# Retention attention and a top-2 router on one core: decay moved from the outputs to q and k, a router cut into thirty steps

## The chip, the cores and the metric

The kernel runs on one core of one Trainium2 chip. The time is that of the device in microseconds (us), from one launch to its end. The profiler takes one more execution, which is longer than a plain one; its times are used here to see where time goes, not how much there is of it.

The engines have short names: PE is TensorE's matmul, PEld its weight load, DVE is VectorE, ACT is ScalarE, POOL is GpSimd, SP is the engine that issues most DMAs. Each engine runs its own list of instructions in order and waits for the others through semaphores.

## The reference

The attention part has 8 batches, 8 heads, 576 positions, 64 wide. The mixture of experts takes its output as 4608 tokens of 512.

```python
scores = q @ k.T / 8                                  # per batch and head
gamma  = 1 - 2 ** (-5 - head)
Dmat   = where(i >= j, gamma ** (i - j), 0)           # i: query position, j: key position
x      = (scores * Dmat) @ v                          # -> [4608, 512]

noisy  = x @ w_gate + log1p(exp(x @ w_noise)) * noise
top2   = the two largest of 8 experts for each token; weights = softmax over the two
out[t] = sum over the two experts e of weight * relu(x[t] @ w1[e]) @ w2[e]
```

The decay `gamma ** (i - j)` splits into a factor for the query and a factor for the key, so it needs no matrix of its own: only the mask `i >= j` has to be applied to the scores.

## The kernel before, in words

**Attention.** The work is cut into 16 units: a unit is half of the heads (four) of one batch, 512 of the 576 positions; four units make a group, which is two batches with all heads (1152 tokens). The last 64 positions of both batches of a group form a "tail", done after the units of the same heads. The loop over `n` from 0 to 16 has a unit `u = n` that begins and a unit `p = n - 1` that ends. Its calls, in order, are: scores of the first pair of heads (`scores(u, 0)`), the output of the unit before (`out(p)`), the transposes of the next unit's q (`tr(u + 1, "q")`), the scores of the second pair, the cast of unit `u + 2` (`cast`), the transposes of the next k, the scores of the tail where there is one (`scores_tail`), the running states of the unit (`states`), and the output of the tail (`out_tail`). Raw q, k and v come from memory four units ahead.

**Casts.** The float32 inputs become bf16 in `cast`: k on POOL by two `affine_select` (L194), v on POOL by a product with a table of key decays (L199), q on ACT with the factor 1/8 (L203). The tails do the same (`cast_tail`, L215 to L221). The query's decay is put on at the end: `out` multiplies what stands in PSUM with the table `gt` on DVE as it copies it to `xT` (L326), two instructions in each unit; `out_tail` does so for the tail (L351).

**Scores.** PE writes the scores of two heads to two PSUM tiles of the name `S` (of which there are just two buffers), and DVE multiplies each with the mask as it copies it out (L270). `scores_tail` takes buffers of the same name, one for each head, one after the other (L336, L337).

**Router.** At the end of each group `route(bp)` begins. It is a generator: each call of `step()` in the attention loop (seven in a pass) lets it run to its next `yield`, so its instructions are put between those of the attention on every engine's list. It computes the gate logits on PE (L489), copies them (L494), takes exp and log on ACT (L496, L497), finds the two largest experts on DVE with some fifty small instructions, counts tokens for each expert (POOL L543, PE L576 and L578), builds one-hot matrices on DVE (L642 to L652), from which PE makes the lists of tokens (L658), and writes the rows of tokens with their weights to the DRAM tensor `xd` (POOL L636). Nine `row(c)` calls transpose the tokens back for that (PE L483, ACT L484). It has some twenty steps.

**Experts.** `early` computes five expert tiles (256 tokens each), for which three of the four groups are enough. It is created when the third route is done; from pass 16 on its pieces alternate with the steps of the route that still runs. When the fourth route is done, the rest of the tiles follow in `experts`, 35 of them, which is mainly a stream of matmuls (L942, L961) fed by gathers on POOL (L823).

The order of the instructions on each engine is the order of these calls: the scheduler is told to keep it for all five engines.

```python
def step():
    while pend and next(pend[0], pend) is pend:
        pend.pop(0)
        routed.append(0)
        if len(routed) == 3:
            work.append(early(tc, K, at, keep, xd, yd, W, EARLY, routed))
    if n == NU:
        more()
```

Of the kernel before, what the change touches and what calls it, by code (L numbers as in the profile page):

```python
# [16 lines left out]
P = 128  # L17
# [26 lines left out]
HD = 64  # L44
NC9 = 9
# [58 lines left out]
def decay_tables(nc, cp, tmp):  # L104

    vg = cp.tile([P, 2, 2, 4, 2], F32, name="vg")
    vgt = cp.tile([P, 8], F32, name="vgt")
    gt = cp.tile([P, 4, 576], F32, name="gt")
    tv = tmp.tile([P, 576], F32, name="tv", bufs=1)
    nc.gpsimd.iota(tv[:, :512].rearrange("p (c r q) -> p c r q", c=4, r=4), pattern=[[P, 4], [1, 4], [4, 32]],  # L110
                   base=0, channel_multiplier=0, allow_small_or_imprecise_dtypes=True)
    nc.gpsimd.iota(tv[:, 512:], pattern=[[1, HD]], base=512, channel_multiplier=0,
                   allow_small_or_imprecise_dtypes=True)
    sv = tmp.tile([P, 2, 2], F32, name="sv")
    nc.gpsimd.iota(sv, pattern=[[256, 2], [1, 2]], base=0, channel_multiplier=2,
                   allow_small_or_imprecise_dtypes=True)
    st = tmp.tile([P, 1], F32, name="st")
    for b in range(2):
        nc.gpsimd.iota(st[b * HD:(b + 1) * HD], pattern=[[0, 1]], base=512, channel_multiplier=1,
                       allow_small_or_imprecise_dtypes=True)  # L120
    for h in range(8):
        lng = math.log(1.0 - 2.0 ** (-5.0 - h))
        hp, hi = h // 2, h % 2
        s = slice(hi * HD, (hi + 1) * HD)
        nc.scalar.activation(vg[:, h // 4, :, h % 4, :], sv, Act.Exp, scale=-lng)
        nc.scalar.activation(vgt[:, h:h + 1], st, Act.Exp, scale=-lng)
        nc.scalar.activation(gt[s, hp, :], tv[s], Act.Exp, scale=lng)
    return vg, vgt, gt


class Attention:
# [26 lines left out]
    def tables(self):  # L158
        self.vg, self.vgt, self.gt = decay_tables(self.nc, self.cp, self.bf)
        for t in self.Tb:  # L160
            self.nc.gpsimd.memset(t, 0.0)
# [24 lines left out]
    def cast(self, u):  # L186

        nc = self.nc
        d = self.u[u]
        hq = self.unit(u)[1]  # L190
        kn = self.bf.tile([P, 2, 2, 4, HD], BF16, name="kn", bufs=3)
        rk = d.pop("rawk").rearrange("p c h (r d) -> p (c h) r d", r=2)
        for r in range(2):
            nc.gpsimd.affine_select(kn[:, r].rearrange("p c h d -> p (c h) d"), rk[:, :, r, :],  # L194
                                    pattern=[[0, 8], [0, HD]], base=1, channel_multiplier=0,
                                    compare_op=Alu.is_gt, fill=0.0)
        vn = self.bf.tile([P, 2, 2, 4, HD], BF16, name="vn", bufs=3)
        rv = d.pop("rawv").rearrange("p c h (r d) -> p (c h) r d", r=2)
        nc.gpsimd.tensor_tensor(vn.rearrange("p r c h d -> p (c h) r d"), rv,  # L199
                                self.vg[:, hq].rearrange("p c h r -> p (c h) r").unsqueeze(3).to_broadcast(  # L200
                                    [P, 8, 2, HD]), Alu.mult)
        qb = self.bf.tile([P, 4, 4, HD], BF16, name="qb")
        nc.scalar.activation(qb.rearrange("p r h d -> p h r d"),  # L203
                             d.pop("rawq").rearrange("p c h w -> p (c h w)").rearrange("p (h r d) -> p h r d", h=4, r=4),
                             Act.Copy, scale=0.125)
        d.update(kn=kn, vn=vn, qb=qb)

    def cast_tail(self, bp):
        nc = self.nc
        d = {}  # L210
        for n in "qk":
            t = self.bf.tile([P, DM], BF16, name=n + "t", bufs=1)
            a = self.tails.pop((n, bp)).rearrange("p h d -> p (h d)")
            if n == "q":
                nc.scalar.activation(t, a, Act.Copy, scale=0.125)  # L215
            else:
                nc.gpsimd.affine_select(t, a, pattern=[[0, DM]], base=1, channel_multiplier=0,
                                        compare_op=Alu.is_gt, fill=0.0)
            d[n] = t
        t = self.bf.tile([P, 8, HD], BF16, name="vt")  # L220
        nc.gpsimd.tensor_tensor(t, self.tails.pop(("v", bp)), self.vgt.unsqueeze(2).to_broadcast([P, 8, HD]), Alu.mult)  # L221
        d["v"] = t
        self.tails[bp] = d

    def tr_tail(self, bp):
# [3 lines left out]
        for hp in range(4):  # L229
            for j, n in enumerate("qk"):  # L230
                nc.tensor.transpose(pt[:, hp, j, :], d[n][:, hp * P:(hp + 1) * P], self.K["ident"])
# [65 lines left out]
    def out(self, u):  # L297
# [17 lines left out]
        for e in range(2):  # L315
# [9 lines left out]
            gv = self.gt[:, 2 * hq:2 * hq + 2, :512].rearrange("p y (c e t) -> p y c e t", c=2, e=2)[:, :, :, e, :]  # L325
            nc.vector.tensor_tensor(xv, p[e], gv, Alu.mult)  # L326

    def scores_tail(self, bp, hp):
        nc = self.nc
        t = self.tails[bp]  # L330
        T = t["T"][:, hp]
        S = self.sp.tile([P, 2, P], BF16, name=f"St{hp % 2}")
        for h in range(2):
            s = slice(h * HD, (h + 1) * HD)
            p = self.ps.tile([P, P], F32, name="S", bufs=2)
            nc.tensor.matmul(p, lhsT=T[s, 1, :], rhs=T[s, 0, :], start=True, stop=True)  # L336
            nc.vector.tensor_tensor(S[:, h, :], p, self.K["maskt"].rearrange("p r q -> p (r q)"), Alu.mult)  # L337
        t["S", hp] = S

    def out_tail(self, bp, hp):  # L340
        nc = self.nc
        t = self.tails[bp]
        p = self.ps.tile([P, 2, HD], F32, name="x", bufs=2)
        for h in range(2):
            s = slice(h * HD, (h + 1) * HD)
            nc.tensor.matmul(p[s].rearrange("p b t -> p (b t)"), lhsT=t["v"][:, 2 * hp + h, :], rhs=t["S", hp][:, h, :],
                             start=True, stop=False, skip_group_check=True)
        for b in range(2):
            nc.tensor.matmul(p[:, b, :], lhsT=self.T.pop((bp, b, hp))[:, 3, :], rhs=t["T"][:, hp, 0, b * HD:(b + 1) * HD],
                             start=False, stop=(b == 1), skip_group_check=True)  # L350
        nc.vector.tensor_tensor(self.xT[bp][:, hp, 8, :].rearrange("p (b t) -> p b t", b=2), p,  # L351
                                self.gt[:, hp, 512:].unsqueeze(1).to_broadcast([P, 2, HD]), Alu.mult)
# [80 lines left out]
class Router:  # L433
# [36 lines left out]
    def route(self, bp):  # L470
# [15 lines left out]
        pg = ps.tile([P, C, 2 * E], F32, name="R", bufs=1)  # L486
        for c in range(C):
            for di in range(KD):
                nc.tensor.matmul(pg[:, c, :], lhsT=xT[:, di, c, :], rhs=self.wgn[:, di, :],  # L489
                                 start=(di == 0), stop=(di == KD - 1))  # L490
            if c == 4:
                yield
        lg = sp.tile([P, C, 2 * E], F32, name="lg")
        V.tensor_copy(lg, pg)  # L494
# [3 lines left out]
        row(0)  # L498
        yield
        row(1)  # L500
        V.tensor_mul(nl[:, :8], nl[:, :8], self.noise[:, 2 * bp:2 * bp + 2].rearrange("p b c e -> p (b c) e"))
        V.tensor_mul(nl[:, 8], nl[:, 8], self.noiset[:, bp])
        V.tensor_add(nl, nl, lg[:, :, :E])
# [18 lines left out]

        m1, w1 = first_max(nl, "a")
        yield
        row(2)
# [3 lines left out]
        V.scalar_tensor_tensor(nl2, M1, -1.0e30, nl, Alu.mult, Alu.add)  # L529
        m2, w2 = first_max(nl2, "b")  # L530
        yield
        row(3)
# [11 lines left out]
        yield  # L544
        row(4)
# [4 lines left out]
        r = col("r")  # L550
        V.tensor_scalar_add(r, d, 1.0)
        V.reciprocal(r, r)
        V.tensor_mul(d, d, r)
        low1 = col("low1")
        V.tensor_tensor(low1, w1, w2, Alu.is_gt)
        df = col("df")
        V.tensor_sub(df, r, d)
        V.tensor_mul(df, df, low1)
        yield


        pl = sp.tile([P, C, PLW], F32, name="pl")
        V.memset(pl[:, :, 7], 0.0)
        V.tensor_add(pl[:, :, 1], d, df)
        V.tensor_sub(r, r, df)
        V.tensor_sub(pl[:, :, 2], r, pl[:, :, 1])
        V.tensor_scalar(pl[:, :, 0], w[:, 1], -1.0, float(E), Alu.mult, Alu.add)
        V.tensor_copy(pl[:, :, 3], K["tok"][:, bp])
# [5 lines left out]
        yield  # L574
        pr = ps.tile(SH, F32, name="R", bufs=1)
# [4 lines left out]
        row(5)  # L580
        yield

        prf = sp.tile(SH, F32, name="prf", bufs=1)
        V.tensor_tensor(prf, pr, self.fill.unsqueeze(1).to_broadcast(SH), Alu.add)
        V.tensor_mul(pd, M, prf)
        rk = sp.tile([P, C, 2], F32, name="rk")
# [5 lines left out]
        V.tensor_reduce(rc, pd, AX, Alu.add)  # L592

# [10 lines left out]
        yield  # L604
        row(6)
        lo = sp.tile([P, 2, C], BF16, name="lo")
        V.tensor_copy(lo, lh[:, 0])
        hi = sp.tile([P, 2, C], F32, name="hi")
        V.tensor_copy(hi, lh[:, 1])

        key = self.keep["key"][:, :, c0:c0 + C]
        V.tensor_scalar(key, w, -KEY, KEY * E + 1.0, Alu.mult, Alu.add)
# [611 lines left out]
```

## The time and the profile before

| what | value |
|---|---|
| time, median of 3 runs | 549.66 us (549.3 to 552.47) |
| span of the profiled execution | 597.5 us |
| PE busy | 454.6 us (76%) |
| DVE, ACT, POOL busy | 277.8, 268.2, 274.3 us (45% to 46%) |
| granted PE clock, mean | 0.847 |
| first transposes of attention | at 15.95 us |
| attention's last pass ends | at about 211 us |
| first matmuls of the remaining expert tiles | at 261 us |

The average share of an engine says little here, as the kernel has stages with different limits: 16 passes of attention with the router between them, then the last route beside the early expert tiles, then the experts. A pass can be found in the trace by its first score matmuls (L264): they start at 19.0, 28.3, 34.4, 42.0 and 48.1 us for passes 0 to 4, and at 55.4, 67.2, 87.7, 96.6 and 103.9 us for passes 5 to 9. The first route begins at the end of pass 4.

### The profile page before, as it was taken

The page shows a single profiled execution, that of the slowest core. Times are in us where ns is not written, and L with a number is a line of the kernel's source. Part 1 is how long each engine was busy: PE and PEld are TensorE (multiplying, and loading weights), DVE is VectorE, ACT ScalarE, POOL GpSimd, SP SyncE. Part 2 cuts the span into 40 slices and gives each one's busy share as a digit, 9 for nine tenths or more (in the row PEclk, how much of TensorE's full clock was granted, in tenths as well). Part 3 has the DMA queues.
Part 4 walks back from the last instruction along what each step waited for, and adds up shares of the span by engine and source line. Part 5 has one row for each costly group of instructions (what it writes and reads, how often), then busy time and mean ns, then how long its engine had stood idle before and what let it go on. Part 6 is the DMA issues. An engine that isn't in the chain of part 4 may idle for free.

```text
span 597.5 us, 11717 instructions
## 1 busy us (share of the span) xinstructions
PE 454.6 (76%) x4587; PEld 315.4 (53%) x4627; DVE 277.8 (46%) x770; ACT 268.2 (45%) x381; POOL 274.3 (46%) x350
## 2 busy tenths in 40 slices
PE   0687738828756678968998799799798798989960
PEld 0565626616644455645665366366464464656630
DVE  0266796796778278313333143243233243344430
ACT  5657716723660365534563464464444451312200
POOL 8753543335232605570246216336347256666660
PEclk9989758655875697988999699799799698999995
DMA  9995999709446313730677567577575643544450
GB/s 239 285 238 119 249 297 265 223 0 259 73 72 130 92 41 125 261 118 17 219 257 251 164 218 235 173 253 232 183 269 183 218 135 114 166 129 130 146 176 20
DMA packets 96170, 104.18 MB, mean 174 GB/s; under 512 B 25447, under 2 KB 73065, under 8 KB 96112
## 3 DMA queue, kind: packets, MB, share of 16 engines
q1 hardware_dynamic: 79824, 69.51, 39.4%
q0 software_dynamic: 15232, 32.84, 20.0%
q10 hardware_dynamic: 1056, 1.05, 0.5%
q8 instruction: 37, 0.61, 0.4%
q14 instruction: 21, 0.17, 0.1%
HBM read 84.66 MB, written 28.72 MB: 190 GB/s over the span
## 4 chain that ended last, share of the span: by engine, by line
PE 25%; issue 17%; POOL 5%; DMA 3%; DVE 2%; another core or an unknown queue 1%; POOLq 0%; ACT 0%; DVEq 0%; ACTq 0%
PE p L942 13%; PE po L961 11%; POOL xg L823 3%; DMA xg<-xd,xi 2%; PE pt L926 1%; POOL out_dram L1003 1%; POOL prv L969 1%; DVE o L997 1%; DMA raw_q<-xd,xi 0%; DMA out_dram<-o,ix 0%; DVE hT L949 0%; ACT xgT L929 0%; POOLq L823 0%; ACT hT L947 0%
## 5 line engine op out<-in xcount | busy, mean ns | idle before, releaser
L942 PE MATMUL p<-xgT,w 128*128 128x256 bf16 x1120 | 223.7, 283 | 18.2 <-issue 13.4
L961 PE MATMUL po<-w,hT 128*128 128x512 bf16 x525 | 205.3, 395 | 11.2 <-issue 9.7
L942 PEld LDWEIGHTS <-w 128*128 128x128 bf16 x1120 | 112.8, 101 | 98.8 <-issue 31.8
L949 DVE TENSOR_SCALAR hT<-p 128x512 bf16<-128x512 f32 x70 | 48.3, 691 | 195.3 <-PE p L942 106.0
L947 ACT ACTIVATE hT<-p 128x512 bf16<-128x512 f32 x70 | 41.8, 597 | 173.6 <-remote 62.9
L1003 POOL DMA_INDIRECT out_dram<-o,ix x45 | 45.7, 1016 | 113.3 <-DVE o L997 98.8
L823 POOL DMA_INDIRECT xg<-xd,xi x64 | 66.0, 1032 | 19.2 <-issue 18.6
L961 PEld LDWEIGHTS <-hT 128*128 128x128 bf16 x560 | 56.3, 100 | 26.1 <-issue 17.4
L969 POOL DMA_INDIRECT prv<-yd,ix x45 | 45.6, 1014 | 39.5 <-issue 39.5
L270 DVE TENSOR_TENSOR S<-S,mask 128x512 bf16<-128x512 f32 x64 | 41.1, 683 | 38.5 <-PE S L264 38.5
L892 ACT ACTIVATE w<-wst 128x1024 bf16<-128x1024 f32 x48 | 47.8, 1048 | 0.0
L292 ACT ACTIVATE Tb<-T 64x512 bf16<-64x512 f32 x32 | 18.8, 589 | 44.7 <-PE T L286 44.4
L194 POOL TENSOR_SCALAR_AFFINE_SELECT kn<-raw_k 128x512 bf16<-128x512 f32 x32 | 24.4, 786 | 26.5 <-issue 10.0
L929 ACT ACTIVATE xgT<-pt 128x1024 bf16<-128x1024 bf16 x35 | 35.7, 1020 | 1.6 <-PE pt L926 1.6
L199 POOL TENSOR_TENSOR vn<-raw_v,vg 128x1024 bf16<-128x1024 f32 x16 | 30.9, 1933 | 5.5 <-DMA raw_v<-in_v_dram 1.5
L997 DVE SCALAR_TENSOR_TENSOR o<-po,g,prv 128x512 f32<-128x512 f32 x45 | 31.7, 742 | 3.0 <-DMA prv<-yd,ix 1.7
L336 PE MATMUL S<-TT 64*128 64x128 bf16 x32 | 7.1, 231 | 31.4 <-DVE S L270 20.1
L543 POOL TENSOR_TENSOR cum<-cum,M 128x16 bf16<-128x16 bf16 x36 | 7.8, 217 | 49.8 <-DVE d L548 47.3
L249 PE MATMUL tr<-ident,qb 128*128 128x128 bf16 x128 | 14.1, 277 | 21.4 <-ACT qb L203 16.3
L484 ACT ACTIVATE xr<-tr 128x512 bf16<-128x512 bf16 x36 | 21.2, 598 | 12.6 <-PE tr L483 9.3
L636 POOL COPY xr<-pl 128x24 f32<-128x24 f32 x12 | 12.1, 1048 | 28.1 <-issue 18.8
L251 ACT ACTIVATE QT<-tr 128x1024 bf16<-128x1024 bf16 x16 | 16.4, 1023 | 18.9 <-PE tr L249 18.9
(205 smaller groups left out, 678.6 us busy)
## 6 DMA issues: line engine op xcount, KB each, us to landing
wst<-in_moe_w_dram SPq DMA_DIRECT2D x48, 512.0 KB
raw_k<-in_k_dram SPq DMA_DIRECT2D x32, 256.0 KB
raw_v<-in_v_dram SPq DMA_DIRECT2D x32, 256.0 KB
yd<-y SPq DMA_DIRECT2D x16, 512.0 KB
raw_q<-in_q_dram SPq DMA_DIRECT2D x14, 512.0 KB
xd<-xr SPq DMA_DIRECT2D x12, 396.0 KB
w<-in_moe_w_dram POOLq DMA_DIRECT2D x4, 1024.0 KB
yd<-raw_v SPq DMA_DIRECT2D x5, 512.0 KB
```

Of the source, the lines that this page charges most:

```text
L199: nc.gpsimd.tensor_tensor(vn.rearrange("p r c h d -> p (c h) r d"), rv, self.vg[:, hq].rearrange("p c h r -> p (c h) r").unsqueeze(3).to_b ...
L270: nc.vector.tensor_tensor(S, p[h], self.K["mask"].unsqueeze(1).to_broadcast([P, 2, 2, P]), Alu.mult)
L823: tc.nc.gpsimd.indirect_dma_start(out=xg[:, s, :], out_offset=None, in_=xd[:, :], in_offset=IOff(ap=keep["xi"][:, j:j + 1], axis=0), bound ...
L892: nc.scalar.activation(W[e][:, k * F:(k + 1) * F], t, Act.Copy)
L929: return lambda: nc.scalar.activation(xgT, pt, Act.Copy)
L942: nc.tensor.matmul(p1[:, f2, :], lhsT=w[:, o:o + P], rhs=xgT[:, di, :], start=(di == 0), stop=(di == KD - 1))
L947: nc.scalar.activation(hT[:, 2 * fp:2 * fp + 2, :], p1, Act.Relu)
L949: V.tensor_relu(hT[:, 2 * fp:2 * fp + 2, :], p1)
L961: nc.tensor.matmul(po[s], lhsT=hT[:, fi, s * P:(s + 1) * P], rhs=w[:, o:o + DM], start=(fi == 0), stop=(fi == KF - 1))
L969: nc.gpsimd.indirect_dma_start(out=prv[i % NP][:, s, :], out_offset=None, in_=yd[:rows, :], in_offset=IOff(ap=st[i]["ix"][:, s, 1:2], axis=0),
L997: V.scalar_tensor_tensor(o[:, s, :], st[i]["po"][s], st[i]["g"][:, s:s + 1], prv[i % NP][:, s, :], Alu.mult, Alu.add)
L1003: ins = nc.gpsimd.indirect_dma_start(out=out[:, :], out_offset=IOff(ap=st[i]["ix"][:, s, 0:1], axis=0), in_=st[i]["o"][:, s, :], in_offset ...
```

## The change

Four things change.

1. The query's decay is put on q, and the key's decay on k instead of v, when they are cast. Both are counted from the middle of the sequence (position 288), so that no factor becomes large. The cast of k and that of q become one product each on POOL (for the first two units on DVE), and v is only copied, on ACT. Then nothing is left to be multiplied in `out`: of the two copies from PSUM one is done by ACT and one by DVE. The large table `gt` is not needed any more.
2. The tail's scores and outputs are done for two pairs of heads at once: two DVE instructions in place of four, and one copy on ACT in place of two products on DVE.
3. The router is cut into about thirty steps, and its work is put in another order. Some small instructions go from DVE to POOL (the row's fields `pl`, the overflow keys `key`), and the one-hot matrices are made in two halves.
4. The gate weights are kept as the sum of two bf16 parts, which makes the gate logits more exact: the matmuls are 32 wide in place of 16, and DVE adds the two halves.

The tables for the decay and the zeros of `Tb` are made before the constants, and `Tb` is cleared by DVE.

```diff
     def cast(self, u, eng=None):
...
-        for r in range(2):
-            nc.gpsimd.affine_select(kn[:, r].rearrange("p c h d -> p (c h) d"), rk[:, :, r, :],
...
+        eng.tensor_tensor(kn.rearrange("p r c h d -> p (c h) r d"),
...
-        nc.gpsimd.tensor_tensor(vn.rearrange("p r c h d -> p (c h) r d"), rv,
...
+        nc.scalar.activation(vn.rearrange("p r c h d -> p (c h) r d"),
+                             d.pop("rawv").rearrange("p c h (r d) -> p (c h) r d", r=2), Act.Copy)
...
-        nc.scalar.activation(qb.rearrange("p r h d -> p h r d"),
...
+        eng.tensor_tensor(qb.rearrange("p r h d -> p h r d"),
...
     # out
-            nc.vector.tensor_tensor(xv, p[e], gv, Alu.mult)
+            if e:
+                nc.vector.tensor_copy(xv, p[e])
+            else:
+                nc.scalar.activation(xv, p[e], Act.Copy)
...
     # scores_tail, out_tail
-        for h in range(2):
-            p = self.ps.tile([P, P], F32, name="S", bufs=2)
...
+        p = [self.ps.tile([P, 2, P], F32, name="S", bufs=2) for h in range(2)]
...
-        nc.vector.tensor_tensor(self.xT[bp][:, hp, 8, :].rearrange("p (b t) -> p b t", b=2), p,
-                                self.gt[:, hp, 512:].unsqueeze(1).to_broadcast([P, 2, HD]), Alu.mult)
+        nc.scalar.activation(self.xT[bp][:, 2 * hq:2 * hq + 2, 8, :], p.rearrange("p y b t -> p y (b t)"), Act.Copy)
...
     # route
-        V.tensor_copy(lg, pg)
+        V.tensor_copy(lg, pg[:, :, 1])
+        V.tensor_add(lg, lg, pg[:, :, 0])
...
-        V.memset(pl[:, :, 7], 0.0)
-        V.tensor_add(pl[:, :, 1], d, df)
...
+        G = nc.gpsimd
+        G.memset(pl[:, :, 7], 0.0)
+        G.tensor_tensor(pl[:, :, 1], d, df, Alu.add)
...
-        V.tensor_tensor(olo.rearrange("p a c l -> p (a c) l"), K["iota"].unsqueeze(1).to_broadcast(sh),
...
+        for j in range(2):
+            sh = [P, C, P]
+            V.tensor_tensor(olo[:, j], K["iota"].unsqueeze(1).to_broadcast(sh),
...
+            yield
...
-        V.tensor_add(key, key, rc.rearrange("p c a -> p a c"))
+        G.tensor_tensor(key, key, rc.rearrange("p c a -> p a c"), Alu.add)
...
-        at.cast(0)
+        at.cast(0, nc.vector)
+        nc.gpsimd.tensor_copy(wgn[:, :, 0], wg32)
+        nc.gpsimd.tensor_tensor(wgn[:, :, 1], wg32, wgn[:, :, 0], Alu.subtract)
```

## The prediction, made before the changed kernel had run

> **What bounds the kernel now.** I read first the busy time by stage. The columns are the stretch (us), its length, then busy time and instruction count of PE, PEld, DVE, ACT and POOL, the granted PE clock, the DMA share and GB/s. The first three rows are, roughly, passes 4 to 7, 8 to 11 and 12 to 15; then come the last route and the experts:
>
> ```profile
> 49.80:98.00 48.20, 30.98 (x600) 24.77 (x598) 38.83 (x102) 26.18 (x37) 22.75 (x29) 0.72 0.97 257
> 98.00:149.00 51.00, 33.52 (x542) 26.48 (x539) 40.10 (x105) 24.96 (x36) 20.68 (x26) 0.59 0.65 166
> 149.00:201.00 52.00, 31.61 (x588) 24.78 (x586) 37.57 (x106) 22.15 (x32) 17.31 (x27) 0.70 0.51 92
> ...
> 211.00:259.00 48.00, 39.11 (x310) 26.18 (x312) 31.56 (x111) 26.42 (x44) 21.30 (x27) 0.93 0.40 138
> 259.00:597.00 338.00, 282.27 (x1925) 184.49 (x1959) 109.00 (x297) 133.00 (x177) 152.53 (x152) 0.91 0.54 176
> ```
>
> In the three stretches with a route DVE is busiest (38 to 40 us of about 50), though its share over the whole span is 46%. The experts are a PE stage, and the change doesn't touch them. So I cut the first route's stretch into its passes 5, 6, 7 and 8:
>
> ```profile
> 55.40:67.20 11.80, 8.00 (x163) 6.50 (x160) 7.43 (x25) 9.07 (x15) 4.85 (x13) 0.83 0.75 200
> 67.20:87.70 20.50, 9.01 (x147) 6.73 (x146) 19.61 (x55) 6.90 (x11) 10.94 (x12) 0.58 1.00 256
> 87.70:96.60 8.90, 8.19 (x146) 7.12 (x144) 6.82 (x12) 4.41 (x6) 5.04 (x4) 0.65 1.13 325
> 96.60:103.90 7.30, 5.90 (x156) 4.54 (x154) 5.25 (x12) 5.72 (x8) 2.83 (x3) 1.00 0.94 219
> ```
>
> DVE has 19.6 of pass 6's 20.5 us: the router's load falls into one pass. Passes 7 and 8 follow PE, with 2 us of DVE free in each. Pass 5 follows no busy engine; there ACT's list (exp, a table load of 1.28 us, log) stands ahead of the copies that PE waits for. PE's waits in passes 5 to 15 (us in total, times, longest) say the same:
>
> ```profile
> PE S L336 <- DVE S L270: 18.0, 10, 6.3
> PE S L336 <- DVE St L337: 10.3, 5, 3.3
> PE S L264 <- DVE S L270: 6.1, 6, 3.0
> PE tr L249 <- ACT xr L484: 5.2, 3, 2.1
> ```
>
> PE waits for a buffer `S` that DVE reaches late, behind router work: 34 us. Last, the timeline of pass 10 (start, us, engine, line):
>
> ```profile
> 116.14 0.58 DVE L557 TENSOR_TENSOR df<-r,d 128x9 f32<-128x9 f32 x1
> ...
> 116.68 1.90 POOL L199 TENSOR_TENSOR vn<-raw_v,vg 128x1024 bf16<-128x1024 f32 x1
> 116.75 1.85 DVE L558 TENSOR_TENSOR df<-df,low 128x9 f32<-128x9 f32 x1
> ```
>
> Nine elements take 1.85 us instead of 0.17 (the shortest of that line), and end with POOL's product: POOL's casts hold DVE up.
>
> **What the Trainium skill says.** "GPSIMD Engine Reference", Specifications: its SBUF interfaces are shared with VectorE, in contention with DVE instructions with two SBUF inputs or in a two-port mode. The trace agrees (L558 above). "VectorE: DVE Perf Modes", Why PSUM operands drop a tier: float32 from PSUM gets one element a cycle at most, so a plain copy is as dear as a product. The trace has 0.682 us for the product L326 and 0.691 for the one-input L949. "TensorE: Matmul & The Clock Gate", What's actually happening: PE's clock halves after an idle window. The trace agrees: 1.00 in pass 8, 0.58 in pass 6. So shorter waits pay a little twice; I put no number on that.
>
> **The change part by part**, for a group of four passes unless said otherwise.
>
> *Outputs.* DVE does one copy of 0.69 (row L949) in each pass instead of two of 0.682 (L326): 4 x (1.364 - 0.69) = 2.7 us less. ACT gets a copy of 0.60 (row L947) in each pass: +2.4.
>
> *Tails.* DVE's eight L337 (0.286) and four L351 (0.288) were 3.44 us. Four instructions of 256 elements remain. Between 0.286 at 128 and 0.683 at 512 elements a line gives 0.42 each, 1.67 in all: 1.8 us less. ACT gets two small copies, about 0.4 each.
>
> *Router on DVE.* Where the last route runs undisturbed, the six `pl` instructions take 0.65 us start to start (225.16 to 225.81), L631 to L633 0.38, the four `key` ones 0.88, and one of L622/L624 goes: 2.1 less. Added: one sum for the two gate halves, 0.3 (as L494); four more instructions by halving the one-hots, about 0.06 each. Net 1.5 us less. DVE so loses 2.7 + 1.8 + 1.5 = **6.0 us** of a group's 38 to 40, which lie on the path in the passes that DVE bounds.
>
> *Smaller steps.* By the order of the new program the router's DVE work is spread over four passes: with the router-free base of 3.4 us (four masks and a copy) I count, without blocking, 7.1, 9.3, 11.0 and 5.7 us (the tails included) for passes 5 to 8, against PE's 8.0, 9.0, 6.5 and 8.5. The peak of 19.6 goes. What it can fill is the DVE time free in passes 7 and 8: **4 us**.
>
> *Casts on POOL.* k was 2 x 0.63 undisturbed, v 1.93; now k and q are two products of the shape of L199, 2 x 1.93 = 3.87. So POOL holds the shared interface 0.7 us longer a pass, and the router's DVE work now meets it in nearly every pass. The lines of route 0 that were blocked (L557, L589, L647 and three short ones) lost some 4.5 us. I take 6, so **+1.5**; the bounds are 0 and +4.5 (twice as much). POOL's casts rise by 4 x 0.7, the tail's two products by 0.4, and a dozen router instructions of about 0.2 come: from 20-23 to 27-29 us, under the 45 of a group. Its list has casts behind router instructions that wait for DVE. I count the q cast for the next pass ready about when pass 7 starts, some 2 us ahead of its transposes: close, but hidden. ACT trades q's cast for v's (1.05 both).
>
> *ACT's queue.* In pass 5 and 6 ACT (9.07 busy in pass 5) gets the copies besides its table load, and the transposes' copies are behind them: **+2**.
>
> Sum for a group: -6.0 - 4 + 1.5 + 2 = **-6.5**, three groups -19.5.
>
> *The end of attention.* The third route is now done in pass 16, so `early` starts later: its first four matmul groups (5.56 us at half clock in pass 16) move behind, where they take 4.2 at full clock; in return PE's waits of 3.61 and 2.12 us in the last route (for DVE `M` and POOL `cum`) find work in front of them. The gather for the first early tile stands ahead of the tail in PE's list, as before (3.2 us of waiting, now perhaps 5). Net **-1.5**. On POOL's list only five gathers instead of nine stand between the clearing of the second and of the third tile for `experts`: 4 x 1.31 = 5.2 us earlier. PE waits there 1.26, 0.91 and 1.86 us (266.6 to 271.4): **-3.5**.
>
> *The start.* PE's first transposes wait until 15.95 us for q's cast behind the decay tables on ACT; DVE's cast (an estimate from VectorE: DVE Perf Modes, the errata section's fp32 formula: 1175 cycles, 1.22 us; POOL's 1.93 is the upper bound) can come earlier. But the loads run at 230 to 308 GB/s, DMA share above 1, until pass 3, and POOL waits for raw k at 23.1 us. So this gain is lost at the first DMA wait. The tail's products (1.04 each, behind 3.87 of casts on POOL) delay the tail's transposes in pass 0 by 1.5: **+1.5**, between -3 and +3.
>
> *Gate halves.* 36 matmuls in a group, 32 wide instead of 16. They took 170 ns (L489), those 64 wide 217 (L286): between 0 and 36 x 47 ns = 1.7 us. I take nothing, as PE waits for DVE in that stage.
>
> Total in the profile: -19.5 - 1.5 - 3.5 + 1.5 = -23.0 us. A plain run is 549.66/597.5 = 0.92 of the profiled span; I scale: -21.2, thus **528.5 us**.
>
> **The rivals.** *A, DVE stays blocked.* POOL's two products keep DVE's router work waiting (+4.5 instead of +1.5), and the smaller steps fill nothing: the group gives -6.0 + 4.5 + 0 = -1.5. In the profile -4.5 - 1.5 - 3.5 + 1.5 = -8, times 0.92: 542. For it: L558 and L568 both blocked in a row in pass 10. Against: masks and copies from PSUM were not blocked (L270's mean is 683 ns).
>
> *B, PE's waits nearly go.* All PE gaps above 0.7 us in passes 5 to 15 sum to 45 us; if two thirds go and the clock recovers 5, -35 - 5 + 1.5 = -38.5, times 0.92: 514. For it: PE needs only 31 to 34 of the 50 us. Against: DVE still has 33 and more.
>
> *C, POOL becomes the bound.* The casts come too late behind router instructions that wait for DVE, and PE waits 2.5 us for q or k in each of 12 passes: -23 + 30 = +7, times 0.92: **556**, slower. For it: POOL already waited 31.5 us for DVE at L543, with casts behind it. Against: three buffers of `kn` and the cast two passes ahead.
>
> **How the numbers follow.** Forecast 0.50, A 0.20, B 0.18, C 0.12. The forecast's own unknowns (blocking 0 to +4.5 a group, start -3 to +3) are about -6 to +10 us around 528.5. For 8 in 10 the range reaches from 511 (B with a little to spare) to 549 (A with its start at the bad end); C is left out. Faster by over 1% (under 544.2): nearly all of the forecast and B, and most of A: 0.80. C is slower but for a small part: 0.11. Within 1%: 0.09.
>
> **What would show it.** Right: no pass with DVE near 100% of 20 us, passes 5 to 16 at 10 to 13 us each, PE's waits for `S` (the matmuls that are now L336 and L264) under 15 us in all; DVE busy in a group about 33 to 36 us; the third tile's wait gone. Wrong: small DVE router instructions of 1.8 us in most passes (A); PE transposes waiting for POOL's `qb` or `kn` (C); the last route longer than 48 us; the start later by more than 3 us.

## The result, and the profile after

The changed kernel takes 528.0 us (median of 4 runs, 527.3 to 529.3), the kernel before 550.9 beside it: a ratio of 0.959, with a 95% interval of 0.955 to 0.963. The forecast was 528.5 us.

One thing has to be said ahead of all comparisons. The first profile of the kernel before (597.5 us) was long in the expert stage alone: 338 us from the first transposes of the remaining tiles to the end, against 290 in the profile after. A profiled execution is not longer as such: the profile after spans 526.5 us, in an execution of 528.4. The experiments below ran on three chips. On two of them that stage took 325 to 345 us in every kernel, and the plain runs of the kernel before took 600 to 604 us (medians); on the third they took 549.6 us again. So times in us are not compared between chips. I compare ratios to the kernel before on the same chip, and for the attention the moment at which the first transposes of the remaining expert tiles begin, which hardly depends on the chip: 259.0 us before and 236.7 after in the first two profiles, 261.7 and 238.5 on the two chips with the long stage. That is 22 to 23 us, as much as the plain runs gained.

The busy time by stage of the changed kernel (stretch, length, then busy us and instructions of PE, PEld, DVE, ACT, POOL, granted PE clock, DMA share, GB/s) answers to the first view of before. The rows are passes 5 to 8, 9 to 12 and 13 to the end of attention, the last route, and the experts:

```profile
53.00:101.30 48.30, 33.49 (x596) 26.46 (x596) 39.72 (x80) 29.95 (x45) 28.48 (x37) 0.68 1.00 294
101.30:150.00 48.70, 32.61 (x605) 25.88 (x605) 38.61 (x85) 28.84 (x43) 28.27 (x38) 0.68 0.55 128
150.00:191.50 41.50, 26.83 (x482) 20.84 (x482) 28.25 (x81) 19.94 (x32) 15.61 (x36) 0.66 0.48 92
191.50:236.70 45.20, 42.25 (x368) 30.19 (x369) 30.26 (x99) 30.34 (x50) 26.02 (x44) 0.97 0.34 109
236.70:526.50 289.80, 263.73 (x1960) 181.81 (x1959) 110.20 (x300) 133.51 (x177) 155.72 (x155) 0.96 0.65 214
```

DVE has fewer instructions in a group than before (80 to 85 where it had over 100) and yet is just as busy: 39.7 and 38.6 us. Cut into passes 5, 6, 7 and 8:

```profile
53.00:64.50 11.50, 8.43 (x148) 6.91 (x150) 7.91 (x16) 8.70 (x14) 3.95 (x3) 0.65 0.97 284
64.50:75.20 10.70, 7.53 (x156) 5.69 (x156) 10.11 (x31) 8.96 (x15) 5.51 (x17) 0.82 0.95 262
75.20:84.50 9.30, 6.14 (x134) 4.93 (x133) 9.09 (x20) 7.39 (x11) 8.36 (x11) 0.84 1.07 329
84.50:101.30 16.80, 11.39 (x168) 8.94 (x167) 12.61 (x16) 4.89 (x7) 10.67 (x8) 0.52 1.02 302
```

The peak of 20.5 us in pass 6 is gone, but pass 8 has grown from 7.3 to 16.8 us, and the four passes together take 48.3 us against 48.5. What PE waits for in passes 5 to 16 (us in total, times, longest):

```profile
PE R L663 <- DVE oh L652: 13.7, 6, 4.6
PE tr L482 <- ACT QT L244: 8.3, 3, 3.0
PE S L257 <- DVE S L263: 6.4, 4, 3.2
```

Before, PE waited 34 us for the scores' buffers `S`; of that 6.4 us are left. In its place PE stands in front of the second nine of the 18 matmuls L663, which stand on its list right behind the one-hot matrices that they read, with the attention's transposes and scores behind them.

### The profile page after: what moved, and what is told of

The parts are those of the page before. It is cut to its first block, busy times and chain, and to the rows that moved or that the text cites. A ratio compares the mean times of both kernels' runs of the same rounds, so it can differ in the third digit from the quotient of the medians.

```text
span 526.5 us, 11719 instructions
## 1 busy us (share of the span) xinstructions
PE 428.2 (81%) x4627; PEld 308.0 (58%) x4627; DVE 272.3 (52%) x696; ACT 275.7 (52%) x413; POOL 286.6 (54%) x377
## 4 chain that ended last, share of the span: by engine, by line
PE 61%; DVE 15%; DMA 6%; ACT 5%; SPq 4%; issue 3%; POOL 3%; POOLq 0%; DVEq 0%; ACTq 0%
PE p L947 23%; PE po L966 22%; DVE S L263 3%; PE pt L931 3%; SPq L174 2%; PE S L392 2%; PE x L402 2%; DMA raw_q<-xd,xi 2%; PE T L279 2%; DVE olo L643 1%; DVE oh L650 1%; DVE oh L647 1%; SPq L466 1%; DVE oh L652 1%; PE R L663 1%
## 5 line engine op out<-in xcount | busy, mean ns | idle before, releaser
L947 PE MATMUL p<-xgT,w 128*128 128x256 bf16 x1120 | 214.2, 276 | 1.6 <-DVE hT L954 1.6
L966 PE MATMUL po<-w,hT 128*128 128x512 bf16 x560 | 211.3, 382 | 0.0
L947 PEld LDWEIGHTS <-w 128*128 128x128 bf16 x1120 | 111.0, 99 | 74.0 <-issue 3.6
L954 DVE TENSOR_SCALAR hT<-p 128x512 bf16<-128x512 f32 x70 | 48.3, 691 | 145.4 <-PE p L947 145.4
L1008 POOL DMA_INDIRECT out_dram<-o,ix x45 | 45.6, 1012 | 62.1 <-DVE o L1002 47.6
L828 POOL DMA_INDIRECT xg<-xd,xi x64 | 65.5, 1024 | 19.2 <-issue 14.7
L966 PEld LDWEIGHTS <-hT 128*128 128x128 bf16 x560 | 55.1, 98 | 7.8
L263 DVE TENSOR_TENSOR S<-S,mask 128x512 bf16<-128x512 f32 x64 | 41.1, 683 | 33.6 <-PE S L257 33.4
L192 POOL TENSOR_TENSOR kn<-raw_k,kg 128x1024 bf16<-128x1024 f32 x14 | 27.2, 1940 | 29.6 <-PE T L279 15.2
L200 POOL TENSOR_TENSOR qb<-raw_q,qg 128x1024 bf16<-128x1024 f32 x14 | 30.3, 2165 | 0.0
L257 PE MATMUL S<-QT,KT 64*64 64x128 bf16 x512 | 17.6, 260 | 11.8 <-DVE S L263 6.6
L482 PE MATMUL tr<-ident,xT 128*128 128x128 bf16 x144 | 17.3, 256 | 11.0 <-ACT QT L244 8.3
L279 PE MATMUL T<-vn,kn 64*64 64x64 bf16 (+2 forms) x512 | 25.2, 243 | 0.0
L242 PE MATMUL tr<-ident,qb 128*128 128x128 bf16 x128 | 13.7, 270 | 12.8 <-DVE qb L200 12.8
L244 ACT ACTIVATE KT<-tr 128x1024 bf16<-128x1024 bf16 x16 | 16.3, 1018 | 13.3 <-PE tr L242 13.3
```

The costliest lines, as they stand in the source:

```text
L263: nc.vector.tensor_tensor(S, p[h], self.K["mask"].unsqueeze(1).to_broadcast([P, 2, 2, P]), Alu.mult)
L279: nc.tensor.matmul(p[h * HD:(h + 1) * HD, hp, n, :], lhsT=d["kn"][:k, r, c, 2 * hp + h, :], rhs=m, start=(c == 0 and k == P and r == 0 and ...
L828: tc.nc.gpsimd.indirect_dma_start(out=xg[:, s, :], out_offset=None, in_=xd[:, :], in_offset=IOff(ap=keep["xi"][:, j:j + 1], axis=0), bound ...
L947: nc.tensor.matmul(p1[:, f2, :], lhsT=w[:, o:o + P], rhs=xgT[:, di, :], start=(di == 0), stop=(di == KD - 1))
L954: V.tensor_relu(hT[:, 2 * fp:2 * fp + 2, :], p1)
L966: nc.tensor.matmul(po[s], lhsT=hT[:, fi, s * P:(s + 1) * P], rhs=w[:, o:o + DM], start=(fi == 0), stop=(fi == KF - 1))
```

## The experiments

Pass starts and the experts' start are read from each trace by the first matmul concerned. "Held up" is worked out from the trace: for each DVE instruction between 53 and 200 us its duration less the shortest of the same line and tiles, summed. What is left, the sum of the shortest durations, is called DVE's own work below.

| kernel | ratio to before (95%) | pass 5 starts | 5 to 8 | 9 to 12 | 13, 14 | 15 to experts | experts start | held up |
|---|---|---|---|---|---|---|---|---|
| before, first profile | 1 | 55.4 | 48.5 | 53.1 | 30.5 | 71.6 | 259.0 | 15.7 |
| before again | 1 | 55.5 | 51.2 | 53.1 | 30.5 | 71.4 | 261.7 | 16.2 |
| casts, outputs, tails alone | 1.008 (1.005 to 1.010) | 58.5 | 50.7 | 53.7 | 28.9 | 72.9 | 264.6 | 23.6 |
| router alone | 0.967 (0.959 to 0.974) | 54.3 | 51.2 | 50.2 | 20.7 | 73.0 | 249.3 | 14.2 |
| changed, first profile | 0.959 (0.955 to 0.963) | 53.0 | 48.3 | 48.6 | 20.4 | 66.4 | 236.7 | 20.0 |
| changed, control | 0.959 (0.955 to 0.963) | 53.7 | 47.8 | 48.2 | 19.7 | 69.2 | 238.5 | 19.7 |
| coarse steps | 0.965 (0.959 to 0.970) | 53.3 | 46.3 | 46.0 | 23.9 | 68.0 | 237.5 | 15.8 |
| small instructions on DVE | 0.980 (0.976 to 0.984) | 53.1 | 53.6 | 53.3 | 20.9 | 71.9 | 252.7 | 29.5 |
| the same, and q on DVE | 0.968 (0.965 to 0.970) | 54.0 | 48.6 | 49.1 | 20.1 | 67.3 | 239.0 | 14.6 |
| q on DVE | 0.955 (0.949 to 0.960) | 52.7 | 48.4 | 48.0 | 19.2 | 71.1 | 239.4 | 13.1 |
| two more steps | 0.950 (0.941 to 0.958) | 52.7 | 46.9 | 47.0 | 20.3 | 69.8 | 236.7 | 20.5 |
| first casts on POOL | 0.961 (0.958 to 0.963) | 53.3 | 47.5 | 48.7 | 20.0 | 66.7 | 236.2 | 20.2 |
| third tile in its own buffer | 0.946 (0.943 to 0.948) | 53.3 | 47.4 | 47.2 | 19.7 | 67.3 | 234.9 | 20.1 |
| three edits together | 0.935 (0.933 to 0.937) | 54.4 | 47.0 | 45.6 | 19.9 | 66.7 | 233.6 | 14.3 |

### Before again

> The kernel before once more, for its profile alone. My theory now: its first profiled execution (597.5 us) was long in the expert stage only (336 us there against 288 in the changed kernel). Expected: a span of about 550 us, the remaining expert tiles still beginning at 261 us and taking about 288. If the span is again near 597, the profiler stretches the whole kernel before, and the 22 us that the attention gained in the profile must be scaled down.

The time was 607.8 us, with 344.5 us in the experts, so the expected span of 550 didn't come; but other kernels had the same long expert stage on this chip, and the attention ended where it did in the first profile. The profiled execution of before had not been stretched evenly: its experts were slow, its attention was not. Nor does the profiler make the difference: the plain runs of before on this chip took 598 to 608 us too. On which chip the first profile was taken is not on record.

### The two halves of the change

```diff
 # casts, outputs, tails alone: the changed kernel, with
+    the old route() and the old gate weights
 # router alone: the kernel before, with
+    the new route(), the gate weights in one part
```

> Parts 1 and 2 and the start alone: casts, outputs and tails as in the changed kernel, the router and the gate weights as before. Theory R (the prediction's sums): outputs and tails give -4.5 us a group, POOL's casts and ACT's queue take +3.5 back, the start +1.5: about 549 us, 2 below before. Rival C: the three groups gained mainly through the outputs, the tails and the start (-3), and the router's new steps only moved the load from pass 6 to pass 8: about 538 us, more than half of the whole gain of 23.

> Part 3 alone: the router's thirty steps and its new order, with casts, outputs, tails and gate weights as before. Theory R: -5.5 us in each of three groups, -5 at the end of attention: about 529 to 531 us. Rival C: passes 5 to 8 take as long as before (48 us), only the spread of the third route into the last pass helps: about 543 us.

The casts, outputs and tails alone are a loss of 0.8%. Theory R is nearer, and rival C's gain of 12 us is out. The router alone has the ratio that R expected, but the trace sides with C on where it lies: passes 5 to 8 are as long as before (51.2), and of the 14.0 us gained up to pass 15 9.8 lie in passes 13 and 14 (30.5 to 20.7). There the third route's costly part has moved out of pass 14 (DVE 17.5 us busy before, 7.8 now) into passes 15 and 16. The stretch from pass 15 to the experts is only 1.6 us longer for it. Why it costs so little there is not shown: the first matmuls of `early` come at 196.5 us, after the one-hot matrices' (186.6 to 191.4 us).

At the experts' start the halves give +2.9 and -12.4 us, together -9.5, and the whole change -23.2 (control against before again). So about 14 us belong to neither half alone; in the ratios it is 1.6 points (1.008 times 0.967 is 0.975, against 0.959), some 9 of 550 us. The more exact gate weights are in neither half, but they only add work. By stage these 14 us are 3.5 before pass 5, 2.9 and 2.6 in the groups 5 to 8 and 9 to 12, and 5.3 from pass 15 on.

### Two more steps ahead of the matmuls

```diff
+        for _ in range(2 if bp < 3 else 0):
+            yield
         pT = ps.tile([P, 2 * NH], F32, name="R", bufs=1)
```

> The changed kernel with two more empty steps between the last one-hot matrices and the 18 matmuls that read them (in the first three routes). In the changed kernel PE stands 4.4 us in pass 8 and 4.7 in pass 12 in front of the second half of these matmuls, with the attention's work behind them. Theory R (DVE's total amount bounds a group): the wait moves to the scores, the time stays at 528 us within 2. Rival C (it is the place in PE's list): about 4 us less in passes 8 and 12 and 2 in pass 16, so 518 to 522 us.

The waits moved: of PE's 13.7 us for the one-hots 5.1 were left, and the wait for the masks rose from 6.4 us to 12.8:

```profile
PE S L257 <- DVE S L263: 12.8, 12, 3.5
...
PE R L665 <- DVE oh L652: 5.1, 4, 2.1
```

Pass 15 begins 2.4 us earlier than in the control, and the experts 1.8 us, on another chip. By the waits most of it was what R says, as 6.4 of the 8.6 us came back in front of the scores, and a smaller part the place in the list (C). The ratio doesn't decide: its interval overlaps with the control's and takes in most of what C's 518 to 522 us mean (0.942 to 0.950).

### The control, and q's product on DVE

> The changed kernel once more, as the control for the runs beside it. On the chip that ran the experiments so far the rest after attention takes about 340 us in every kernel, against 290 where the changed kernel was first measured, so times in us don't compare between chips: expected a ratio to before of 0.955 to 0.962, and the first transposes of the remaining expert tiles at 237 us of the span, as in the first profile.

```diff
-        eng.tensor_tensor(qb.rearrange("p r h d -> p h r d"),
+        nc.vector.tensor_tensor(qb.rearrange("p r h d -> p h r d"),
```

> The changed kernel with the product for q on DVE in every unit (in the first two units it lasts 1.28 us there) and only k's on POOL. Theory B (what the smaller DVE list ought to give is eaten because POOL's product, 2.17 us on average, holds DVE's router work up): 5 us more DVE work in a group, but 5 us or more of blocked time go: 0 to 4 us faster than the changed kernel. Rival R (DVE's own amount bounds the groups): 3 to 5 us a group slower, 9 to 15 in all.

The control came as expected. With q on DVE, DVE is held up 13.1 us in place of 19.7. The nine products of q between 53 and 200 us add 10.9 us to its list, so that it is busy longer (116.6 us in that stretch in place of 111.8). The experts start at 239.4 us, 0.9 later, and the ratios overlap. That is next to theory B's lower end; R's 9 to 15 us didn't come, though DVE has more to do.

### Coarse steps

```diff
         row(0)
-        yield
...
         V.tensor_mul(pd, M, prf)
-        yield
```

(Four more in the same manner. The changed route has 26 steps; the edit takes out six boundaries, where the text below says seven, and leaves 20.)

> The changed kernel with seven of the router's step boundaries taken out (after row(0), row(1), nl2, thr, prf, rc; 19 steps are left, the order within them stays). The step 'smaller steps fill 4 us a group' of the prediction gives +12 us over the changed kernel. Rival N: the number of steps matters little, since the new order and the halved one-hot matrices stay: within 3 us of it.

The peak moves back to passes 6 and 7 (16.0 and 13.2 us), pass 8 falls to 6.2, and the four passes together take 46.3 us in place of 47.8; passes 13 and 14 take 4.2 us more. The experts start at 237.5 us, 1.0 earlier than in the control. The interval of the ratio lies 0.6% higher, with an overlap. Rival N: the number of steps gives nothing that these runs can tell, certainly not 12 us.

### The small router instructions back on DVE

```diff
-        G = nc.gpsimd
+        G = nc.vector
```

> The changed kernel with its thirteen small router instructions (pl, py, key) back on DVE. The prediction's term: about 2 us of DVE work a group come back, +1 to +2 us a group where DVE bounds, so +4 to +6 us. Rival P: these instructions on POOL held POOL's casts and DVE up in their turn, so nothing is lost: within 2 us of the changed kernel, or faster.

This is the large one: the experts start 14.2 us later than in the control. The prediction had 2 us of DVE work in a group for it. DVE's timeline in pass 7 (start, us, engine, line, operation, tile) shows what happens instead:

```profile
82.94 0.17 DVE L630 CAST hi<-lh 128x18 f32<-128x18 int32 x1
83.02 1.88 DVE L632 TENSOR_SCALAR e<-w 128x18 f32<-128x18 f32 x1
84.93 1.83 DVE L633 TENSOR_TENSOR hi<-hi,e 128x18 f32<-128x18 f32 x1
86.79 1.83 DVE L634 SCALAR_TENSOR_TENSOR hi<-ov,hi 128x18 f32<-128x18 f32 x1
88.65 1.83 DVE L636 TENSOR_SCALAR hib<-hi 128x18 bf16<-128x18 f32 x1
```

and POOL's at the same time:

```profile
82.50 0.48 POOL L624 COPY xr<-pl 128x24 f32<-128x24 f32 x3 [5.65 <-DVE pl L621]
82.95 1.92 POOL L192 TENSOR_TENSOR kn<-raw_k,kg 128x1024 bf16<-128x1024 f32 x1
84.83 1.90 POOL L200 TENSOR_TENSOR qb<-raw_q,qg 128x1024 bf16<-128x1024 f32 x1
86.69 1.90 POOL L192 TENSOR_TENSOR kn<-raw_k,kg 128x1024 bf16<-128x1024 f32 x1
88.55 1.90 POOL L200 TENSOR_TENSOR qb<-raw_q,qg 128x1024 bf16<-128x1024 f32 x1
```

POOL had waited 5.65 us for the last `pl` instruction, which is now DVE's, with two units' casts behind it. Then four products run without a gap. In each of them DVE gets just one instruction of 18 elements done, and it ends with the product: four instructions that need 0.18 us each take 7.4. PE waits 7.0 us for the mask behind them (from 85.4 us on), and 8.5 us in the next group; in the control the waits at these places are 2.6 and 3.5 us.

```diff
-        G = nc.gpsimd
+        G = nc.vector
...
-        eng.tensor_tensor(qb.rearrange("p r h d -> p h r d"),
+        nc.vector.tensor_tensor(qb.rearrange("p r h d -> p h r d"),
```

> The changed kernel with the thirteen small router instructions back on DVE, as in the kernel 14 us slower than the control at the end of attention (252.7 against 238.5 us), and the product for q on DVE as well. Theory B (the 14 us are small DVE instructions that each wait for a whole POOL product): half of POOL's products are gone, so half or more of the 14 us comes back: 243 to 247 us. Rival R (they are DVE's own amount): DVE gets 5 us a group more on top: 258 us or later.

This *adds* 14 products of 1.33 us on average, 19 us, to DVE's list, and yet the experts start at 239.0 us, 13.7 earlier (2.8 later than in the kernel with the first casts on POOL, which ran on the same chip). The ratio recovers 1.2 of the 2.1 points; PE's wait for the third expert tile, which comes later, is longer in this run (4.82 us in place of 3.40). DVE's same lines, now with half as many products on POOL:

```profile
82.32 1.88 DVE L632 TENSOR_SCALAR e<-w 128x18 f32<-128x18 f32 x1
84.24 0.18 DVE L633 TENSOR_TENSOR hi<-hi,e 128x18 f32<-128x18 f32 x1
84.45 0.18 DVE L634 SCALAR_TENSOR_TENSOR hi<-ov,hi 128x18 f32<-128x18 f32 x1
84.66 0.18 DVE L636 TENSOR_SCALAR hib<-hi 128x18 bf16<-128x18 f32 x1
```

One is held up and three are not. That is theory B: what costs here is how many small DVE instructions fall beside a train of POOL products, not how much DVE has to compute. Four runs together show it. With both products on POOL the thirteen instructions on DVE cost 14.2 us (experts at 238.5 and 252.7 us); with q's product on DVE they cost nothing (239.4 and 239.0, the last on another chip). Left open is how the 14.2 us divide between DVE's 13 more instructions and the wait of POOL's list that makes the train.

### The first casts on POOL

```diff
-        at.cast(0, nc.vector)
+        at.cast(0)
...
-        at.cast(1, nc.vector)
+        at.cast(1)
```

> The changed kernel with the casts of the first two units on POOL, as every later one. The prediction said +1.5 us for the start (between -3 and +3); the changed kernel began its first transposes 3.1 us earlier (12.8 instead of 15.95 us). Theory D (DVE's casts brought that): first transposes at about 15 us, of which 1 to 3 us are left at the end of attention. Rival A (the smaller decay tables on ACT brought it: no exp over the 576-wide table): first transposes at about 13.5 us, within 1 us of the changed kernel at the end.

The first transposes now come at 18.3 us, 5.5 later than in the changed kernel, more than either theory said: without DVE's casts the start would be later than before, so it is these that brought the 3.1 us. But the two kernels' first five passes end at the same time. In the changed kernel POOL stands before two casts of pass 4 and 5 and waits for raw k (the time in brackets, and what ended it):

```profile
49.42 1.90 POOL L192 TENSOR_TENSOR kn<-raw_k,kg 128x1024 bf16<-128x1024 f32 x1 [6.50 <-DMA raw_k<-in_k_dram]
...
59.08 1.90 POOL L192 TENSOR_TENSOR kn<-raw_k,kg 128x1024 bf16<-128x1024 f32 x1 [5.89 <-DMA raw_k<-in_k_dram]
```

Passes 0 and 4 take 9.9 and 9.8 us here, and 7.8 and 6.7 with the first casts on POOL. Pass 5 begins at 53.3 us with the first casts on POOL and at 53.0 here, the experts at 236.2 and 236.7: the loads set that time (up to 65 us POOL waits 14.4 us for raw k here, 10.3 with the first casts on POOL), and the early start is worth nothing.

### The third tile in its own buffer

```diff
-        for i in range(3):
+        for i in range(2):
             xg = raw.tile([P, 2, 4, P], F32, name="raw_q")...
```

> The changed kernel, only that two instead of three tiles are gathered ahead into the buffers that the early expert tiles have used; the third goes into a buffer of its own. PE stood 3.40 and 1.63 us for the third tile (244.2 and 249.0 us of the changed kernel's span), though the prediction had this wait gone. Theory G (the third tile's gather comes behind the clearing of a buffer that is free late): the two waits go, 3 to 5 us faster. Rival Q (POOL issues gathers at 1.3 us each, and one of them is late in any case): 0 to 1 us.

The ratio falls to 0.946, against 0.961 for the kernel with the first casts on POOL, which ran beside it and whose attention ends as the changed kernel's does: 9 us, twice what theory G expected. PE's timeline of the changed kernel shows the wait:

```profile
239.15 5.08 PE L947 MATMUL p<-xgT,w 128*128 128x256 bf16 x32
247.62 0.38 PE L931 MATMUL pt<-ident,raw_q 128*128 128x128 bf16 x4 [3.40 <-DMA raw_q<-xd,xi]
...
250.59 0.59 PE L947 MATMUL p<-xgT,w 128*128 128x256 bf16 x2 [1.63 <-DVE hT L954]
```

The rest is the clock. Right behind these waits it is at half:

```profile
250.00:254.00 4.00, 3.42 (x13) 1.81 (x13) 1.13 (x2) 0.23 (x1) 0.00 (x0) 0.50 0.01 2
```

The first 10 and the next 50 us of the experts in the changed kernel:

```profile
236.70:246.70 10.00, 6.36 (x48) 4.95 (x47) 0.94 (x3) 3.24 (x4) 8.01 (x9) 0.83 0.82 268
246.70:296.70 50.00, 47.11 (x336) 31.76 (x337) 16.90 (x49) 26.44 (x36) 12.55 (x14) 0.93 0.59 192
```

and with the third tile in its own buffer:

```profile
234.90:244.90 10.00, 8.74 (x82) 7.06 (x82) 3.97 (x15) 4.65 (x6) 7.84 (x8) 1.00 0.76 255
244.90:294.90 50.00, 49.63 (x375) 34.83 (x380) 19.34 (x52) 31.17 (x42) 20.23 (x20) 1.00 0.73 242
```

In the same 60 us PE does 457 matmuls in place of 384. The clock stays at 1.00 where it was 0.83 and 0.93, and the expert stage is 279.8 us long in place of 289.8. From these rows PE's idle time is 6.5 us, and 1.6 with the own buffer; a matmul takes 139 and 128 ns of busy time, which for 384 of them is an estimated 4.4 us. So about half of the 10 us is waiting and half is the slower clock.

### Three edits together

> Three edits to the changed kernel together: the product for q on DVE, two empty steps ahead of the 18 matmuls in the first two routes, the third tile in its own buffer. If they add up: -1 (q), -3 (steps), -3 to -5 (third tile): ratio to before about 0.945. If the first two only move DVE's load about: about 0.952.

The ratio is 0.935 (0.933 to 0.937), 514.4 us where the kernel before took 549.6: 2.6 points below the kernel with the first casts on POOL beside it (0.961; the changed kernel itself did not run on this chip). In the profile PE's wait for the one-hots has fallen to 3.5 us. Against the third tile alone the plain runs show 4.6 us more; the profiled executions (516.9 and 516.5 us) don't, and the experts start 1.3 us earlier, so where the rest lies is not shown.

## Why the prediction came out right

The total was right to half a microsecond, the way to it only in part. That it came so near is luck: the smaller steps (-12 us in three groups) and the third tile (-3.5) gave nothing. What made up for them was not forecast: between the first two profiles pass 13 to the experts gained 15.3 us where 8.0 were taken, and the start 2.4 where a loss of 1.5 was.

**What was right.** The bound: DVE's queue in the groups, with PE waiting for `S`. The outputs and tails are worth little by themselves: my terms of -2.7, -1.8, +1.5 (casts) and +2 (ACT) leave -1 us a group, and the half with the casts alone showed a change of -0.5, +0.6 and -1.6 us in its three stretches. DVE's own work: it falls by 5.6 us in each of the two groups 5 to 8 and 9 to 12 (38.0 to 32.4 and 39.0 to 33.4), where 6.0 was taken; by halves it is 4.3 and 1.5, where 4.5 and 1.5 was taken. ACT's +2: the waits of PE's transposes for ACT rose from 5.2 us (before again) to 12.6 in the control, 2.5 a group. The gate halves: 188 ns a matmul in place of 170, 0.65 us a group, inside the 0 to 1.7. POOL never became the bound (the prediction's rival C): PE waited 0.3 us in all for `qb` of POOL's in the groups of the control.

**The casts' extra blocking, +1.5 us a group: too small.** In the two groups DVE is held up 4.1 and 1.8 us more (6.2 to 10.3 and 6.9 to 8.7); the bound of +4.5 was nearly reached in the first. So DVE was busy only 0.5 and 2.5 us less in all (39.7 to 39.2 and 41.1 to 38.6), near to what rival A feared. Rival A's sum has an error of its own: -6.0 + 4.5 + 0 leaves out ACT's +2. With it a group gives +0.5, the whole -2 in the profile, and A's time is about 548, not 542.

**Smaller steps fill 4 us a group: wrong.** Taking six boundaries away cost nothing at the experts' start. I had seen that the load of one pass would be spread over four, and it was; but PE's wait moved with it, from the scores' buffers to the one-hot matrices (13.7 us in all). Why the time that DVE had free in passes 7 and 8 was not worth its 4 us no run shows by itself.

**The router on DVE, -1.5 us a group: right for DVE's own work, too small for the time.** I priced the moved instructions by what they take undisturbed, 0.65, 0.38 and 0.88 us, 1.9 in all. Taking that move back added just 2.1 us of own work a group, but the holds rose by 4.7 and 3.7 us, and it cost 14.2 us, 4.7 a group, two and a half times the 1.9. The price was not their own duration but what they meet: POOL's trains of products. I had shown this very effect for one line in pass 10 and charged it to the new casts alone, not to the instructions that would no longer be exposed to it. Whether it is also why the two halves give 10 us and the whole 23 is not shown: the new casts raise the holds by 7.4 us with the old router (16.2 to 23.6) and by 5.5 with the new one (14.2 to 19.7), which is far less of a difference than 14 us.

**The groups, -6.5 each.** Between the first two profiles passes 5 to 8 gained 0.2 us, 9 to 12 gained 4.5, 13 and 14 gained 10.1. The sum of -14.8 (-19.1 between before again and the control) is near the -19.5, its division is not: the costly part of a route was only shifted by two passes, and in the third group it fell out of the group's end. The tests that I had set failed accordingly: pass 8 has 16.8 and pass 12 18.3 us (10 to 13 expected), DVE 39.7 and 38.6 us a group (33 to 36).

**The start, +1.5: the wrong sign, no effect.** It came 3.1 us earlier; pass 5 began 2.4 us earlier, but it did so in the experiment without the early start too (53.3 us). DVE's first two q casts took 1.31 and 1.25 us, where 1.22 was estimated. The argument that a gain is lost at the first DMA wait held.

**The third tile, -3.5: it didn't come.** The gather was earlier by somewhat more than I had said (5.2 us): from the first gather to the clearing of the third buffer 12.6 us instead of 18.8. PE arrived earlier too, but by less (10.7 us after the first gather instead of 14.9), and yet it waits 3.40, 0.34 and 1.63 us, where it waited 4.0. What the term had left out is how long the gather takes to land. Before, PE went on 2.9 us after the issue:

```profile
264.92 1.00 POOL L823 DMA_INDIRECT raw_q<-xd,xi  x1 [0.30 <-issue]
```

```profile
267.83 0.38 PE L926 MATMUL pt<-ident,raw_q 128*128 128x128 bf16 x4 [1.26 <-DMA raw_q<-xd,xi]
```

In the changed kernel it is 7.0 us, to 247.62:

```profile
240.58 1.01 POOL L828 DMA_INDIRECT raw_q<-xd,xi  x1 [0.30 <-issue]
```

Between 240.5 and 248.4 us the DMA share is 1.00, three quarters of it on the queue of the experts' weight loads (four of 512 KB were issued from 237.8 us on); before, the share was 0.33 between 264.9 and 269.2 us, and the gathers' queue alone was at work. With 2.9 us after each issue, an estimate from before, the data would have been there at 243.5 and 244.8 us, about when PE came (244.2). No run takes the weight loads away, so that they are what delays the gathers is likely but not shown. Removing the wait was worth 9 us, as the clock pays again: the Trainium skill, "TensorE: Matmul & The Clock Gate", section What's actually happening, says that the clock halves after an idle window, and the rows above agree (0.50 behind the waits, 1.00 without them). I had named this and put no number on it.

**The end of attention, -1.5.** From pass 15 to the experts it was 5.2 us less between the first two profiles and 2.2 in the second pair. Part of the third route now lies there, so the term can't be read off by itself.

**The scaling by 0.92: wrong.** The profile of before was longer than a plain run in its experts, not in the attention. The unscaled -23.0 would have given 526.7 us; the plain gain was 22.9.

## What to carry to other kernels

Price an instruction on DVE by what runs on POOL at that moment: here an instruction of nine or eighteen elements beside a train of POOL products cost a whole product, so first count the small DVE instructions in such places, and move them or half the products elsewhere. When a stage gets faster, look at the first transfer behind it and at what else the DMA engines carry by then: here the gather was issued earlier, fell among weight loads and took longer to land, and the wait of 5.4 us cost nearly as much again in PE's clock. And if two parts of a change act on the same queue, test them together: one half alone made this kernel slower.

## What was not expected of the hardware

The hold works in both directions. In the control a product of POOL's that starts with DVE's one-hot matrix takes 3.09 us instead of 1.90:

```profile
82.64 3.09 POOL L200 TENSOR_TENSOR qb<-raw_q,qg 128x1024 bf16<-128x1024 f32 x1
```

```profile
82.63 1.35 DVE L643 TENSOR_TENSOR olo<-iota,lo 128x1152 bf16<-128x1152 bf16 x1
```

The Trainium skill, "SBUF — State Buffer", section SBUF: two separate sides, calls the ports that both use an exclusive lock for a whole instruction. The traces agree: 1.83 us for 18 elements beside a product of 1.90, and 1.19 us more for a product beside a one-hot of 1.35. Masks and copies from PSUM were spared: the 44 masks L263 of the control took together 0.37 us more than 44 times their shortest, and its 12 copies L319 at most 0.69 us each, where the shortest took 0.67. So were the reductions: 24 of them were held up 0.19 us in all.
